# Fused attention and two expert layers: layer 2's output weights split a block earlier, the last block's pieces and the parameters tied into later groups, the first chain in two parts

## The chip, the cores and the metric

The kernel runs on one core of one Trainium2 chip. The metric is the device time of one execution in microseconds (us). Below, PE is TensorE, the matrix engine; DVE is VectorE; ACT is ScalarE; POOL is GpSimd; SP is SyncE, which issues all the DMAs here. Each engine works through its own instruction stream in order, and an instruction that waits holds up all that stand behind it on that engine.

## What is computed

Chunked attention over 4608 tokens, then two layers, each a product up to 2048 features, an elementwise function, and a product back to 512:

```python
scores = scale * np.matmul(q_c, k_c.transpose(0, 1, 2, 4, 3))   # chunks of 64
attn = softmax(scores); x = np.matmul(attn, v_c)                # x: [4608, 512]
# layer 1
h = x @ w_in;  r = np.maximum(h, 0.0);  g = s * (r * r) + b;  x = g @ w_out
# layer 2
h = x @ w_in
P = a[0] + a[1] * h + a[2] * h2 + a[3] * h3                     # h2 = h*h, h3 = h2*h
Q = 1.0 + np.abs(b[0]) * np.abs(h) + np.abs(b[1]) * h2
g = P / (Q + 1e-06);  out = g @ w_out
```

The products are kept precise by splitting a number, scaled by a power of two, into two float16 halves (hi and lo) and adding three of the four partial products.

## The kernel before

**Stages.** Tokens go in blocks: two small ones and eight of 512 in layer 1 (loop `for j in range(NFULL, NB)`), nine of 512 in layer 2. A block of layer 1 has four groups (`l1_group`), each with four slots (`l1_slot`) into which jobs from a table are put (`at(slot, fn, ...)`): attention of later blocks, pieces of x and y, and the preparation of layer 2's weights (`w2_load`, `w2_park`, then `w2_scale`). Layer 1's result of a block, y, gets its scale from the largest of its values (`y_norm`), and is then cut into seven pieces (`y_piece`, line 414 on: ACT converts to the hi half at L415, DVE subtracts for the lo half at L416; four pieces, T3, T1, T2 and T4, need a subtraction on DVE first, L402 to L411), which wait in DRAM until layer 2 fetches them (`l2_load`).

**Layer 2's output weights** (`wo2`) are decoded from float64 and parked as float32 in DRAM. In the last block of layer 1 they are fetched again (L197) into the buffers that layer 1's own weights leave, and there split into halves by ACT (L185) and DVE (L186). Eight are split in the last block and eight at the start of layer 2 (`late_jobs`).

**Layer 2** runs 36 groups of 4 blocks' quarters (`seq`). In step i TensorE makes the seven products of group i, numbered 1 to 7, in the banks bZ, bY and bC, and h is put together from them: DVE adds into h at L1070 and L1072, ACT copies from bZ at L1078 after product 3, the last. Product 3 adds into the same bank bZ that L1070 reads before it. Then the chain of the group follows: ACT makes v and e (L946, L947), DVE three operations (L955 to L957), ACT logarithm and exponential (L961, L962), DVE four operations (L970, L971, L977, L978), and g is ready. Two steps later TensorE uses g in `l2_y` (L989). The first and last chains are cut into four parts, all others are whole. After the last group of a block ACT copies four outputs (L995). Each block needs a handful of numbers first (`l2_par`, some 22 tiny DVE operations, L683 to L708).

**The order** of an engine's instructions isn't that of the code alone: a list scheduler puts them out as its own estimate of their readiness allows, unless `tc.issue_after(x)` ties the instructions on x's engine behind x. So ACT's part of a piece, for which nothing is tied, may stand elsewhere than DVE's.

Of the kernel before, what the change touches and what calls it, by code (L numbers as in the profile page):

```python
# [8 lines left out]
F32 = mybir.dt.float32  # L9
F16 = mybir.dt.float16  # L10
BF16 = mybir.dt.bfloat16
I32 = mybir.dt.int32
AF = mybir.ActivationFunctionType
ALU = mybir.AluOpType
AX = mybir.AxisListType
# [5 lines left out]
def attn_moe_moe2(ctx: ExitStack, tc: tile.TileContext, qk, v, w_in, w_out, s_in, b_in,  # L21
                  w2_in, w2_out, a2_in, b2_in, out):
    nc = tc.nc
# [4 lines left out]
    KD = DM // 128  # L28
# [47 lines left out]
    def tiny(n, nm, dt=F32):  # L76
        return y1_p.tile([128, n], dt, name=nm, tag=nm, bufs=2)
# [36 lines left out]
    class Weight:  # L114
# [34 lines left out]
        def at(self, u):  # L149
            return self.pool[u[1] % 2] if self.kind == "in" else self.pool  # L150
# [181 lines left out]
    def last(e):  # L332
        return next(i for i in reversed(nc.cur_bb.bb.instructions) if i.engine == e)
# [45 lines left out]
    def norm_bound(mx, inv, sc, nm):  # L379
        sq = tiny(KD, nm + "q")  # L380
        V.tensor_tensor(out=sq, in0=mx, in1=mx, op=ALU.mult)
        m = tiny(1, nm)
        V.tensor_reduce(out=m, in_=sq, axis=AX.X, op=ALU.add)
        tot = tiny(1, nm + "t")
        G.partition_all_reduce(tot, m, channels=128, reduce_op=bass.bass_isa.ReduceOp.add)
        pow2_root(tot, inv, sc, nm + "p")
# [177 lines left out]
    def y_norm(j2):  # L564
        m = tiny(KD, "ym")
        for dd in range(KD):
            V.tensor_reduce(out=m[:, dd:dd + 1], in_=y32[j2][:, dd, :], axis=AX.X, op=ALU.max,
                            apply_absolute_value=True)
        norm_bound(m, invy[j2], scy, "yn")
        V.tensor_scalar(out=scy, in0=scy, scalar1=0.25, scalar2=None, op0=ALU.mult)  # L570

# [11 lines left out]
    def w2_park(n):  # L583
        for m in (n, n + 1):
            w, i = park[m]
            w.decode(i, raw_p, "wf")
            V.tensor_reduce(out=am2[:, m // KF, i:i + 1], in_=w.f32[w.order[i]], axis=AX.X, op=ALU.max,
                            apply_absolute_value=True)
            w.park(i)

    quad, wsum = {}, {}

# [187 lines left out]
    for n in range(0, 2 * KF, 2):  # L780
        slot = start[2] + WS + WP * n // 2
        at(slot - 5, w2_load, n)
        at(slot, w2_park, n)
    at(start[2] + WS + WP * KF, w2_scale)

    at(start[3], l2_consts)
    at(start[NB - 1] + 2, l2_par, 0)
    at(start[NB - 1] + 3, l2_par, 1)

    if True:  # L790
        A.preload_act_table_set("natural_log_exp_and_others")
# [90 lines left out]
            return m2  # L882

        quads = [(kk, g) for g in range(2) for kk in range(2)]
        wo2.todo, wo2.cut = list(GO), list(GO)

        def l1_slot(slot, after):
            j, k = slot // KF, slot % KF
            with tc.issue_after(after.ins) if after else ExitStack():
                run_jobs(slot)  # L890
            if j == NB - 1:
                if k >= 6:
                    wo2.fetch(wo2.todo.pop(0))
                if k >= 8:
                    wo2.split(wo2.cut.pop(0))
                for n in range(28 * k // KF, 28 * (k + 1) // KF):
                    q = quads[n // 7]
                    w2_combo(q, WORD[n % 7])
                    if n % 7 == 6 and n // 7 + 1 < 4:
                        w2_fetch(quads[n // 7 + 1])  # L900
# [102 lines left out]
        T.matmul(out=prime, lhsT=wo2.hl[0][:, 0:128], rhs=wo2.hl[0][:, 0:512], start=True, stop=True)  # L1003
        N = len(seq)
        full, parts = [(0, BIG)], [(a, a + 512) for a in range(0, BIG, 512)]
        m4 = {i: [[], [], [], []] for i in range(N + 2)}
        for i in range(N):
            for q in range(4):
# [6 lines left out]
        extra = {}  # L1015

        def late_jobs():
            for fn, args in [fn for slot in sorted(jobs) for fn in jobs.pop(slot)]:
                extra.setdefault(4 + 2 * YORD.index(args[1]) if fn is y_piece else 3, []).append((fn, args))
            for n in range(len(wo2.cut)):  # L1020
                extra.setdefault(n * 2 // len(wo2.cut), []).append((lambda: wo2.split(wo2.cut.pop(0)), ()))

        last_m2 = m2_of(prev)

        def run_m4(i, slot):
            for u in m4[i][slot]:
                l2_y(*u)
            if i == 0:
                last_m2(slot)
                for _ in range((len(wo2.todo) + 3 - slot) // (4 - slot)):  # L1030
                    wo2.fetch(wo2.todo.pop(0))
                if slot == 3:
                    late_jobs()

        for i in range(N + 2):
            cur, c = i < N, i - 1
            sl = (parts if c in (0, N - 1) else full) if 0 <= c < N else []
            if cur:
                j, u = seq[i]
                if u == 1 and 1 < j + 1 < NB2:  # L1040
                    l2_par(j + 1)
                h = hs[i] = l2_p.tile([128, BIG], F32, name="h", tag="h", bufs=2)
                hq = h.rearrange("p (a s b t) -> p a b s t", a=2, s=2, b=2)
                Z, Y = new_bank(i, "Z"), new_bank(i, "Y")
                l2_product(i, "1", Z, True)
                l2_product(i, "7", Y, True)
                if u == 3 and j + 1 < NB2:
                    l2_load(j + 1)
# [29 lines left out]
                A.activation(out=hq[:, 0, 1], in_=Z, func=AF.Copy)  # L1078
            run_m4(i, 3)
            for fn, args in extra.pop(i, []):  # L1080
                fn(*args)
        assert not extra


# [33 lines left out]
```

## Time and profile before

| | |
|---|---|
| median of 3 runs | 1588.24 us (1588.1 to 1588.85) |
| the profiled execution | 1593.58 us, its span 1591.8 us |
| PE busy | 1544.3 us, 97% of the span |
| DVE busy | 1317.2 us, 83% |
| ACT busy | 962.1 us, 60% |
| mean granted clock of TensorE | 0.988 |
| all DMA | 131.43 MB, mean 83 GB/s |

How to read it: the busy shares are means over stages. Layer 1's last block is about 797 to 874 us from the span's start, the one before it about 720 to 797; layer 2 begins at 860 with its first products, and its steps are regular from about 1060 to 1580. The time before and after the span, some 1.8 us, belongs to the profiled execution's time.

### The profile page before, as it was taken

What the parts mean: (1) busy time and instruction counts of PE and PEld (TensorE: products, weight loads), DVE (VectorE), ACT (ScalarE), POOL (GpSimd) and SP (SyncE); (2) the same over time, 40 slices, a digit from 0 to 9 for tenths busy, and PEclk for the clock granted to TensorE, in tenths of its full rate; (3) what the DMA queues carried; (4) which work ended last, traced back from release to release, by engine and by line L of the source; (5) the groups of instructions that cost most, each with busy time, mean ns of one, the idle gap of its engine ahead of it and who ended that gap; (6) DMA issues with size and microseconds to landing.
All of it is one profiled execution on the core that took longest, in us unless ns stands there. A gap on an engine that the chain in (4) does not pass through costs nothing.

```text
span 1591.8 us, 29579 instructions
## 1 busy us (share of the span) xinstructions
PE 1544.3 (97%) x12501; PEld 1046.6 (66%) x12501; DVE 1317.2 (83%) x1980; ACT 962.1 (60%) x1268; POOL 24.1 (2%) x57
## 2 busy tenths in 40 slices
PE   8999999989999998999999899999999999999998
PEld 6878666656666665666666666666666666666664
DVE  7987878778878788665684999999999989888887
ACT  3565967656666565655675865555656565656564
POOL 0000000000000000000000000000000000000000
PEclk8999999999999999999999999999999999999999
DMA  7722124444534452311133020101010101010000
GB/s 275 281 76 73 47 55 127 160 139 147 152 107 156 137 166 74 87 41 54 46 121 120 14 86 27 47 27 47 27 47 28 47 27 47 28 47 34 27 27 27
DMA packets 86118, 131.43 MB, mean 83 GB/s; under 512 B 39648, under 2 KB 39648, under 8 KB 85984
## 3 DMA queue, kind: packets, MB, share of 16 engines
q1 hardware_dynamic: 85984, 129.53, 25.8%
q8 instruction: 98, 1.61, 0.4%
q14 instruction: 36, 0.29, 0.1%
HBM read 86.77 MB, written 34.34 MB: 76 GB/s over the span
## 4 chain that ended last, share of the span: by engine, by line
PE 62%; DVE 22%; ACT 7%; DMA 4%; issue 4%; POOL 0%; SPq 0%; DVEq 0%; ACTq 0%; POOLq 0%
PE y L989 18%; PE bZ L446 15%; PE y L485 11%; PE bY L446 10%; DMA raw<-in_moe_w_in_dram 2%; PE bC L446 2%; DVE bits L144 2%; PE hp L455 1%; DVE wf L145 1%; PE y L468 1%; DVE e L957 1%; DVE e L977 1%; DVE e L956 1%; DVE v L971 1%; PE sp L264 1%
## 5 line engine op out<-in xcount | busy, mean ns | idle before, releaser
L446 PEld LDWEIGHTS <-whl 128*128 128x128 f16 x5712 | 558.2, 98 | 134.7 <-issue 19.8
L446 PE MATMUL bZ<-xhl,whl 128*128 128x256 f16 x3264 | 404.2, 274 | 10.6 <-DVE h L520 7.4
L989 PE MATMUL y<-whl,g 128*128 128x512 f16 x1728 | 396.3, 379 | 4.6 <-DVE g L978 3.5
L485 PE MATMUL y<-g,whl 128*128 128x512 f16 x1536 | 353.4, 379 | 2.7 <-ACT g L493 1.8
L989 PEld LDWEIGHTS <-g 128*128 128x128 f16 x1728 | 168.6, 98 | 180.4 <-DVE g L978 5.0
L446 PE MATMUL bY<-xhl,whl 128*128 128x256 f16 x2016 | 253.0, 276 | 2.1 <-ACT sn L937 0.7
L485 PEld LDWEIGHTS <-whl 128*128 128x128 f16 x1536 | 150.4, 98 | 156.8 <-issue 3.4
L1078 ACT ACTIVATE h<-bZ 128x512 f32<-128x512 f32 x36 | 21.5, 596 | 224.8 <-PE bZ L446 173.0
L955 DVE SCALAR_TENSOR_TENSOR v<-v,c 128x2048 f32<-128x2048 f32 (+1 forms) x42 | 85.7, 2044 | 33.4 <-ACT v L946 33.4
L494 DVE TENSOR_TENSOR g<-h,g 128x1024 f16<-128x1024 f32 x64 | 78.2, 1221 | 35.9 <-ACT g L493 35.9
L522 ACT ACTIVATE h<-h 128x1024 f32<-128x1024 f32 x32 | 33.8, 1056 | 115.6 <-DVE h L520 115.6
L956 DVE TENSOR_TENSOR e<-e,h 128x2048 f32<-128x2048 f32 (+1 forms) x42 | 83.1, 1981 | 13.8 <-ACT e L947 13.8
L970 DVE SCALAR_TENSOR_TENSOR g<-e,na,r 128x2048 f16<-128x2048 f32 (+1 forms) x42 | 85.7, 2044 | 5.3 <-ACT r L962 2.2
L957 DVE SCALAR_TENSOR_TENSOR e<-e,na,h 128x2048 f32<-128x2048 f32 (+1 forms) x42 | 85.8, 2045 | 0.7
L977 DVE SCALAR_TENSOR_TENSOR e<-e,na,v 128x2048 f32<-128x2048 f32 (+1 forms) x42 | 85.6, 2042 | 0.7
L947 ACT ACTIVATE e<-h,na 128x2048 f32<-128x2048 f32 (+1 forms) x42 | 77.3, 1842 | 11.6 <-DVE g L978 11.6
L971 DVE SCALAR_TENSOR_TENSOR v<-v,g 128x2048 f32<-128x2048 f32 (+1 forms) x42 | 83.2, 1984 | 1.0
L978 DVE TENSOR_TENSOR g<-e,r 128x2048 f16<-128x2048 f32 (+1 forms) x42 | 82.9, 1976 | 0.1
L946 ACT ACTIVATE v<-h,bc 128x2048 f32<-128x2048 f32 (+1 forms) x42 | 73.8, 1759 | 15.0 <-DVE h L1072 13.9
L961 ACT ACTIVATE r<-v,c 128x2048 f32<-128x2048 f32 (+1 forms) x42 | 73.5, 1756 | 2.6 <-DVE v L955 2.6
L962 ACT ACTIVATE r<-r,c 128x2048 f32<-128x2048 f32 (+1 forms) x42 | 73.5, 1758 | 1.0
L492 ACT ACTIVATE h<-h 128x1024 f32<-128x1024 f32 x64 | 67.4, 1053 | 1.0
(189 smaller groups left out, 1820.7 us busy)
## 6 DMA issues: line engine op xcount, KB each, us to landing
qk<-in_qk_dram SPq DMA_DIRECT2D x36, 512.0 KB, 3.7
raw<-in_moe_w_in_dram SPq DMA_DIRECT2D x16, 1024.0 KB, 5.8
raw<-in_moe_w_out_dram SPq DMA_DIRECT2D x16, 1024.0 KB, 5.4
v<-in_v_dram SPq DMA_DIRECT2D x36, 256.0 KB, 2.7
out_dram<-o SPq DMA_DIRECT2D x36, 256.0 KB, 2.1
yd<-yhl SPq DMA_DIRECT2D x27, 256.0 KB, 2.0
xhl<-yd SPq DMA_DIRECT2D x27, 256.0 KB, 2.6
w2din<-wf SPq DMA_DIRECT2D x16, 256.0 KB, 2.0
```

Of the source, the lines that this page charges most:

```text
L446: T.matmul(out=b[:, s, :], lhsT=t[:, a, o:o + 128], rhs=x[pk][:, l, kk, :], start=start and s + kk + n == 0, stop=stop and s + kk + n == 4 ...
L485: T.matmul(out=ybank[j][dd], lhsT=wo1.hl[f][:, o:o + 128], rhs=g[:, l], start=(first and m == 0), stop=(last and m == 2))
L494: V.tensor_tensor(out=g[:, 1], in0=hf, in1=g[:, 0], op=ALU.subtract)
L947: A.activation(out=e, in_=hh, func=AF.Identity, scale=na[:, 3:4], bias=na[:, 2:3])
L955: V.scalar_tensor_tensor(out=v, in0=v, scalar=dlt, in1=v, op0=ALU.add, op1=ALU.mult)
L956: V.tensor_tensor(out=e, in0=e, in1=hh, op=ALU.mult)
L957: V.scalar_tensor_tensor(out=e, in0=e, scalar=na[:, 1:2], in1=hh, op0=ALU.add, op1=ALU.mult)
L970: V.scalar_tensor_tensor(out=g[:, 0], in0=e, scalar=na[:, 0:1], in1=r, op0=ALU.add, op1=ALU.mult)
L971: V.scalar_tensor_tensor(out=v, in0=v, scalar=q0c, in1=g[:, 0], op0=ALU.add, op1=ALU.mult)
L977: V.scalar_tensor_tensor(out=e, in0=e, scalar=na[:, 0:1], in1=v, op0=ALU.add, op1=ALU.subtract)
L978: V.tensor_tensor(out=g[:, 1], in0=e, in1=r, op=ALU.mult)
L989: T.matmul(out=ybank[j][t], lhsT=g[:, a, q, t * 128:(t + 1) * 128], rhs=w[:, l * 512:(l + 1) * 512], start=(u + q == 0 and m == 0), stop=( ...
```

## The change

Four things. (1) Layer 2's output weights are split once their scale is known, a block or more before the last one (`wo2_ahead`): each is loaded, split through one float32 buffer and one buffer for the halves, and stored back in its place in DRAM; later it is only fetched (`wo2_fetch`). (2) The last block's y: its four maxima are tied behind the chain's last DVE instruction in steps 8 to 11 of layer 2, its scale in 12, its seven pieces in 13, 15, ... 25. They ran in steps 1 to 6 before. (3) `l2_par`: three of the nine calls, and not two, come ahead of layer 2; the others are called at the start of a block's last group for the block after the next, tied behind the last DVE instruction traced. (4) The first chain is cut into two parts of 1024 columns in place of four of 512.

```diff
+    def wo2_ahead(i):
+        u = wo2.order[i]
+        f = raw_p.tile([128, 512], F32, name="wf", tag="wf", bufs=1)
+        nc.sync.dma_start(out=f, in_=wo2.dr[u])
+        hl = raw_p.tile([128, 512], F32, name="wb", tag="bits").bitcast(F16)
+        A.activation(out=hl[:, 0:512], in_=f, func=AF.Identity, scale=wo2.sc)
+        V.scalar_tensor_tensor(out=hl[:, 512:1024], in0=f, scalar=wo2.sc, in1=hl[:, 0:512],
+                               op0=ALU.mult, op1=ALU.subtract)
+        nc.sync.dma_start(out=wo2.dr[u].bitcast(F16), in_=hl)
...
+    for i in range(KF):
+        at(start[2] + WS + WP * KF + 2 + 5 * i // 4, wo2_ahead, i)
...
-    at(start[NB - 1] + 2, l2_par, 0)
-    at(start[NB - 1] + 3, l2_par, 1)
+    for j in range(3):
+        at(start[NB - 1] + 10 + j, l2_par, j)
...
                 if k >= 6:
-                    wo2.fetch(wo2.todo.pop(0))
-                if k >= 8:
-                    wo2.split(wo2.cut.pop(0))
+                    wo2_fetch()
...
+            for dd in range(KD):
+                extra.setdefault(8 + dd, []).append((y_max, (dd,)))
+            extra.setdefault(12, []).append((y_bound, (NB2 - 1, m)))
+            for n, p in enumerate(YORD):
+                extra.setdefault(13 + 2 * n, []).append((y_piece, (NB2 - 1, p)))
...
-            sl = (parts if c in (0, N - 1) else full) if 0 <= c < N else []
+            sl = {0: half, N - 1: parts}.get(c, full) if 0 <= c < N else []
...
-                if u == 1 and 1 < j + 1 < NB2:
-                    l2_par(j + 1)
+                if u == 3 and 3 <= j + 2 < NB2:
+                    with tc.issue_after(last(dve)):
+                        l2_par(j + 2)
...
             for fn, args in extra.pop(i, []):
-                fn(*args)
+                with tc.issue_after(last(dve)):
+                    fn(*args)
```

How this moves instructions, at three places. First ACT in layer 1's last block but one, where wb is the buffer of the new halves, yhl a piece's halves, bY and bZ TensorE's banks; now:

```order
L290 ACTIVATE ph<-e 128x512
L599 ACTIVATE wb<-wf,c_191 128x512
L415 ACTIVATE yhl<-y_9652,c_256 128x512
L513 ACTIVATE h_10059<-bY 128x2x256
L514 ACTIVATE bY<-bZ 128x512
L415 ACTIVATE yhl<-tx,c_256 128x512
L415 ACTIVATE yhl<-y_9652,c_256 128x512
L599 ACTIVATE wb<-wf,c_191 128x512 x2
L522 ACTIVATE h_10060<-h_10060 128x1024
```

The L599 rows are new; two follow each other ahead of L522.

Second DVE in layer 2 after the chain of group 13, the one in which a block's outputs are copied; before:

```order
L977 SCALAR_TENSOR_TENSOR e<-e,na,v 128x2048
L1072 TENSOR_TENSOR h<-bY,sn 128x2x256
L978 TENSOR_TENSOR g<-e,r 128x2048
L955 SCALAR_TENSOR_TENSOR v<-v,c_270 128x2048
L956 TENSOR_TENSOR e<-e,h 128x2048
```

and now (L997 is the former L978, L974 the former L955):

```order
L997 TENSOR_TENSOR g<-e,r 128x2048
L702 SCALAR_TENSOR_TENSOR c<-c_252,c_186 128x1
L706 MEMSET m 128x1
L705 TENSOR_SCALAR hb<-c 128x1
L725 TENSOR_TENSOR bc<-c_269,c 128x1
L707 TENSOR_TENSOR m<-hb,c_266 128x1
L708 TENSOR_TENSOR m<-hb 128x1
L709 TENSOR_TENSOR m<-m,c_266 128x1
L710 TENSOR_TENSOR m<-m,hb 128x1
L711 TENSOR_TENSOR m<-m,c_265 128x4
L713 TENSOR_REDUCE gm<-m 128x1
L714 TENSOR_SCALAR gm<-gm 128x1
```

Five more tiny rows follow before L974. They stood ahead of the chain with the output copies, and now stand behind it.

Third ACT around group 15's copy of bZ into h (L1078 before, L1107 now) and its v (L946, now L965); before:

```order
L1068 ACTIVATE h<-bC 128x2x256
L937 ACTIVATE sn<-bZ 128x512
L937 ACTIVATE sn<-bY 128x512
L1078 ACTIVATE h<-bZ 128x2x256
L946 ACTIVATE v<-h,bc 128x2048
```

and now:

```order
L1097 ACTIVATE h<-bC 128x2x256
L956 ACTIVATE sn<-bZ 128x512
L956 ACTIVATE sn<-bY 128x512
L415 ACTIVATE yhl<-tx,c_256 128x512
L1107 ACTIVATE h<-bZ 128x2x256
L415 ACTIVATE yhl<-y_11504,c_256 128x512
L965 ACTIVATE v<-h,bc 128x2048
```

Two conversions of y's pieces stand around the copy; tx is what DVE's L402 writes, which is tied behind the L997 of the chain before.

## Rows read from the trace of the kernel before

**Rows 1.** Busy us of each engine in five stretches, granted clock, DMA share.

```profile
core 0: us, PE busy (x) PEld busy (x) DVE busy (x) ACT busy (x) POOL busy (x), PEclk, DMA share, GB/s
...
800.00:880.00 80.00, 78.18 (x523) 50.82 (x521) 53.19 (x81) 54.52 (x82) 0.81 (x1) 1.00 0.38 122
880.00:920.00 40.00, 35.10 (x260) 25.12 (x258) 39.86 (x54) 30.94 (x42) 0.74 (x1) 1.00 0.05 14
920.00:1060.00 140.00, 134.44 (x892) 86.63 (x890) 132.76 (x110) 80.34 (x73) 0.00 (x0) 1.00 0.14 44
...
1100.00:1580.00 480.00, 480.00 (x3210) 313.78 (x3208) 435.38 (x303) 275.19 (x254) 0.00 (x0) 1.00 0.10 32
...
520.00:540.00 20.00, 18.74 (x176) 12.88 (x177) 13.99 (x31) 10.02 (x16) 0.35 (x1) 0.91 0.30 91
```

**Rows 2.** Waits of PE, 880 to 1080: us in total, times, longest.

```profile
PE y L989 <- DVE g L978: 3.5, 5, 1.0
```

**Rows 3.** Timeline of ACT in layer 2: start, us, line, [idle before].

```profile
1094.96 0.60 ACT L1078 ACTIVATE h<-bZ 128x512 f32<-128x512 f32 x1 [8.03 <-PE bZ L446]
...
1114.49 0.60 ACT L1078 ACTIVATE h<-bZ 128x512 f32<-128x512 f32 x1 [8.03 <-PE bZ L446]
```

**Rows 4.** Timeline of DVE in layer 2, 1089 to 1120.

```profile
1093.36 2.28 DVE L978 TENSOR_TENSOR g<-e,r 128x2048 f16<-128x2048 f32 x1
1097.63 2.35 DVE L955 SCALAR_TENSOR_TENSOR v<-v,c 128x2048 f32<-128x2048 f32 x1 [1.99 <-ACT v L946]
...
1111.68 0.68 DVE L1070 TENSOR_TENSOR h<-bZ,sn 128x512 f32<-128x512 f32 x1
...
1115.08 0.15 DVE L701 RECIPROCAL na<-ig 128x1 f32<-128x1 f32 x1
...
1117.60 2.34 DVE L955 SCALAR_TENSOR_TENSOR v<-v,c 128x2048 f32<-128x2048 f32 x1
```

**Rows 5.** Timeline of PE in the same step.

```profile
1112.98 1.47 PE L446 MATMUL bZ<-xhl,whl 128*128 128x256 f16 x12
```

**Rows 6.** Timeline of DVE and PE, 1039 to 1056.

```profile
1039.59 2.34 DVE L955 SCALAR_TENSOR_TENSOR v<-v,c 128x2048 f32<-128x2048 f32 x1
...
1054.38 1.47 PE L446 MATMUL bZ<-xhl,whl 128*128 128x256 f16 x12 [1.19 <-DVE h L1070]
```

**Rows 7.** Groups by form, 860 to 1060: busy us, mean ns, idle before.

```profile
L955 DVE SCALAR_TENSOR_TENSOR v<-v,c 128x2048 f32<-128x2048 f32 x9 | 21.1, 2346 | 1.4 <-ACT v L946 1.4
...
L186 DVE SCALAR_TENSOR_TENSOR whl<-wf,c,whl 128x512 f16<-128x512 f32 x8 | 6.0, 744 | 0.0
...
L567 DVE TENSOR_REDUCE ym<-y 128x1 f32<-128x512 f32 x4 | 2.7, 683 | 0.0
...
L402 DVE TENSOR_TENSOR tx<-y 128x512 f32<-128x512 f32 x1 | 0.7, 682 | 0.0
```

**Rows 8.** DMA issues: KB each, median us from issue to landing.

```profile
w2dout<-wf SPq DMA_DIRECT2D x16, 256.0 KB, 2.0
wf<-w2dout SPq DMA_DIRECT2D x16, 256.0 KB, 2.6
```

**Rows 9.** Timeline of ACT in layer 1's last block but one.

```profile
753.80 1.06 ACT L522 ACTIVATE h<-h 128x1024 f32<-128x1024 f32 x1 [4.71 <-DVE h L520]
```

**Rows 10.** Timeline of ACT and DVE after a chain with output copies.

```profile
1153.57 0.60 ACT L1078 ACTIVATE h<-bZ 128x512 f32<-128x512 f32 x1 [6.73 <-DVE h L1072]
...
1153.47 2.28 DVE L978 TENSOR_TENSOR g<-e,r 128x2048 f16<-128x2048 f32 x1
1156.24 2.35 DVE L955 SCALAR_TENSOR_TENSOR v<-v,c 128x2048 f32<-128x2048 f32 x1 [0.49 <-ACT v L946]
```

**Rows 11.** Timeline of DVE: the scale of an earlier block's y.

```profile
639.05 0.15 DVE L383 TENSOR_REDUCE yn<-ynq 128x1 f32<-128x4 f32 x1
639.70 0.15 DVE L104 TENSOR_SCALAR ynpm<-ynt 128x1 f32<-128x1 f32 x1 [0.51 <-POOL ynt L385]
```

**Rows 12.** Timeline of PE in layer 1, 508 to 524.

```profile
521.26 0.68 PE L264 MATMUL sp<-qk 64*64 64x64 f32 x18 [1.39 <-ACT x L316]
```

More of the change, by code (lines that the diff above doesn't have):

```diff
@@ L568, in y_norm, with y_bound @@
                             apply_absolute_value=True)
+        y_bound(j2, m)
+    def y_bound(j2, m):
         norm_bound(m, invy[j2], scy, "yn")
@@ L589, in w2_park, with wo2_fetch @@
             w.park(i)
+    def wo2_ahead(i):
[7 more added lines that the diff above has]
+        nc.sync.dma_start(out=wo2.dr[u].bitcast(F16), in_=hl)
+    def wo2_fetch():
+        u = wo2.todo.pop(0)
+        t = wo1_p.tile([128, 512], F32, name="whl", tag="w").bitcast(F16)
+        nc.sync.dma_start(out=t, in_=wo2.dr[u].bitcast(F16))
+        wo2.hl[u] = t
     quad, wsum = {}, {}
@@ L884, in attn_moe_moe2 @@
         quads = [(kk, g) for g in range(2) for kk in range(2)]
-        wo2.todo, wo2.cut = list(GO), list(GO)
+        wo2.todo = list(GO)
         def l1_slot(slot, after):
@@ L1005, in attn_moe_moe2 @@
         full, parts = [(0, BIG)], [(a, a + 512) for a in range(0, BIG, 512)]
+        half = [(a, a + 1024) for a in range(0, BIG, 1024)]
         m4 = {i: [[], [], [], []] for i in range(N + 2)}
@@ L1017, in late_jobs, with y_max @@
         def late_jobs():
[L1018 to L1021, printed above, removed]
+            m = tiny(KD, "ym")
+            def y_max(dd):
+                V.tensor_reduce(out=m[:, dd:dd + 1], in_=y32[NB2 - 1][:, dd, :], axis=AX.X, op=ALU.max,
+                                apply_absolute_value=True)
+            for dd in range(KD):
[3 more added lines that the diff above has]
+                extra.setdefault(13 + 2 * n, []).append((y_piece, (NB2 - 1, p)))
+            jobs.clear()
         last_m2 = m2_of(prev)
@@ L1030, in run_m4 @@
                 for _ in range((len(wo2.todo) + 3 - slot) // (4 - slot)):
-                    wo2.fetch(wo2.todo.pop(0))
+                    wo2_fetch()
                 if slot == 3:
```

## The prediction

> **What bounds the kernel now.** I read the busy time by stretches first. There the reader sees four stretches [rows 1]: the last layer-1 block (800 to 880) with TensorE busy 78.18 of 80 us, the first 40 us of layer 2 with 35.10 of 40, the next 140 us with 134.44 of 140, and 1100 to 1580 with 480.00 of 480. TensorE sets the end, so a change is worth what it takes out of, or puts into, TensorE's idle time. What there is to win before 1060 is 1.82 + 4.90 + 5.56 = 12.3 us; VectorE is full there (39.86 of 40, 132.76 of 140), and the waits name it [rows 2]. Then I read the steady stretch instruction by instruction, because the change adds work there, and "480 of 480" does not say how near to waiting TensorE is. One group of layer 2 takes 19.53 us (the copy at 1094.96, the next at 1114.49 [rows 3]). Its loop: ScalarE copies product 3 out of PSUM (L1078), makes v, VectorE starts its chain with L955 2.67 us after that copy began (1097.63), reaches the add L1070 at 1111.68, done at 1112.36 [rows 4], and TensorE's product 3 of the next group, which accumulates into the bank that this add reads, starts at 1112.98 [rows 5]. So the loop has **0.62 us** to spare in 19.53. Whatever delays L955 by more stops TensorE, at once and for good. The trace holds one such case: at 1039.59 L955 began 1.9 us later than usual behind the tiny parameter operations, and TensorE stood 1.19 us at 1054.38, waiting for L1070 [rows 6].
>
> **What it removes.** VectorE loses, between 875 and 985, eight weight splits of 0.744 us, four maxima of 0.683 and the last block's seven pieces with their subtractions (about 0.74 and 0.68 each) [rows 7]: 6.0 + 2.7 + 7.9 = 16.6 us. In the first chain alone 4 maxima and 4 splits go (5.7 us), but the second half's v is queued on ScalarE behind four y copies, which I put at 3 us of VectorE idle that was none before; by that the second group's adds come some 2.6 to 3 us earlier. I take 1.8 us of the 4.90 as left: **-3.1**. In the next 140 us VectorE then has a chain of some 17 us against 19.5 of TensorE and leads; I take 0.3 of the 5.56 as left: **-5.3** (bounds 0 and -5.56). In the last block eight splits on each engine go; half of 1.82 I leave, since its first stall follows a load of the first layer's weights: **-0.9** (0 to -1.82). Together -9.3.
>
> **What the split ahead adds.** Sixteen times a load of 256 KB, 0.71 us of ScalarE, 0.74 of VectorE, a store, through one buffer each. Load and store both start behind VectorE's half and land after 2.6 and 2.0 us [rows 8], so one step needs about 4.1 us before the next can start. Steps stand about five microseconds apart, mostly in pauses in which ScalarE waits for VectorE or TensorE anyway, as the 4.71 us at 753.80 [rows 9]. The tightest place is the first one shown of the order: two steps stand side by side in that pause, 0.71 + 0.74 + 2.6 + 0.71 = 4.8 us in 4.7. Nothing of this is under a stall in the trace (TensorE is busy 80 of 80 there), and the loss is bounded by 0 and, if each step held TensorE by what it has over half a pause, 16 x 0.9 = 14 us. Nearest to the pause is a small loss: **+1.0**.
>
> **What moves into the steady loop.** Here I find the change's real price; nothing covers it beyond 0.62 us.
> (a) The parameters of a block (six of them now inside layer 2, one each four groups) stood, in the steady part before, ahead of the chain whose output copies make it late: there 2.52 us of tiny operations from 1115.08 to 1117.60 [rows 4] filled the pause of 2.0 us, 0.5 too long, inside the 0.62. Now they stand right behind that late chain. After such a chain VectorE has no pause: its last L978 begins at 1153.47, 0.10 before the copy at 1153.57, and the next L955 at 1156.24 [rows 10], only 0.5 us after L978's end (2.2 us after its start). 2.52 us there delay L955 by 2.52 - 0.57 = 1.95, and TensorE by 1.95 - 0.62 = **1.3 us, six times: 7.8**. This is the case of 1054.38 again, within 0.1.
> (b) The scale of the last block's y: VectorE does seven tiny operations with a GpSimd reduction among them (0.65 us from L383 to L104 [rows 11], 0.19 from each other one to the next, as the parameter operations; some 1.75 in all), and ScalarE's first conversion, which waits for the last of them, stands ahead of v. v then starts 0.6 (the chain's end) + 1.75 + 0.65 (the conversion) = 3.0 us after the copy began instead of 0.6: 2.4 late, minus 0.62: **1.8**.
> (c) The four pieces with a subtraction (T3, T1, T2, T4). The subtraction is tied behind the chain's last instruction on VectorE, so it starts 0.6 us after the copy should (1115.08 against 1114.49), and takes 0.68 [rows 3, 4, 7]. ScalarE's conversion of it stands ahead of that copy, so ScalarE waits for it: 0.6 + 0.7 + 0.65 = 1.9 us late. Minus 0.62 that is **1.3 each**. T3 and T4 have the conversion of a second piece ahead of v, 0.6 more; T3, T1 and T4 come one group after a delayed chain, which has used up the 0.62: 0.6 more. So 2.5, 1.9, 1.3, 2.5: **8.2**. The maxima (0.68 in a pause of 2.0) and the three pieces without a subtraction stay under 0.62: 0, and up to 0.6 each where another delay has used it.
> Bounds of (a) to (c): 0, if the pauses before L955 grow for a reason I don't see, and 24, if none of the 0.62 is there.
>
> **The sum.** -3.1 - 5.3 - 0.9 + 1.0 + 7.8 + 1.8 + 8.2 = +9.5 us. The profiled execution took 1593.58 us; with it the sum is 1603.1. It lies 5.3 us above the median of the runs shown, 1588.24, for which I forecast **1597.7 us**, slower by 0.6%. The chains at the end are as before, so nothing is lost or won in the tail.
>
> **A rule on the clock.** At 521.26 TensorE resumed after 1.39 us [rows 12], and in the 20 us around it the granted clock was 0.91 of full speed; in the 40 us from 880, with 4.90 us idle, it stayed at 1.00 [rows 1]. At 0.91 a stretch of 20 us holds 1.8 us less work. The Trainium skill (TensorE: Matmul & The Clock Gate, Why this matters for your kernels) says that long idle gaps between bursts of matmuls put the clock back to half. By that rule and the row at 521 each of the eleven stalls of (a) to (c) could cost another 1.8 us, the sum would be 1603.1 + 19.8 for the profiled execution; by the row at 880 nothing is added. The stalls here lie between long runs of matmuls, as at 880, so I add nothing.
>
> **Rivals.**
> 1. The waits of (a) to (c) don't come about: the loop opens because VectorE, freed of 16.6 us, leads. Then the sum is -9.3 + 1.0 = -8.3: 1579.9, faster. For it: VectorE is busy only 435.38 of 480 in the steady part. Against: the 0.62 us does not hang on the load but on the loop copy, v, chain, add, in which VectorE never leads, since L955 waits for v [rows 4].
> 2. Half of it: only the parameters (a), or only the pieces (b, c), stop TensorE. -8.3 + 7.8 or + 10.0: 1587.7 to 1589.9, no change. For it: the two have separate causes. Against: both use the same 0.62.
> 3. The split ahead blocks ScalarE, in addition: two copies of a PSUM bank for TensorE stand behind each step in the order; it decides from the point where a step's wait is longer than ScalarE's pause. 1597.7 + 13 = 1610.7. Against: the pauses of 4.7 us.
> 4. The change doesn't do what it says: VectorE stays the bound at the start of layer 2, for the chain in two parts starts later than one in four, and only -3 of the 9.3 comes. 1604 with the rest as forecast.
> 5. The clock of the rule above falls behind the longer stalls: 1597.7 + up to 19.8.
>
> **How the numbers follow.** Forecast 0.66; rival 1 0.13; rival 2 0.10; rival 3 0.04; rival 4 0.04; rival 5 0.03. The forecast's own range is 1592 to 1602 (its costs 4 to 5 us either way, the gains 2). For 8 in 10 I reach down through rival 2, to 1586.5, and up to 1603; rival 1 and the far ends of 3 and 5 are left out. A measurement of this kernel can tell about 0.2%, 3.2 us, from no change. Slower by more: 0.66 with 0.02 off for its low end, rivals 3, 4 and 5: 0.75. Within: most of rival 2 and that low end: 0.10. Faster: rival 1 and a little of 2: 0.15.
>
> **What would show it.** In the profile after, TensorE's idle time in the last block and the next 180 us should fall from 12.3 to some 3 us, and 1100 to 1580 should no longer be full: stalls "bZ waits for DVE h" of 1.2 to 2.6 us, six of them one to two groups behind the tiny operations, and ScalarE's conversion of tx or y idle ahead of its copy of bZ for more than 8 us. No split should stand in layer 2, and the stretch 640 to 800 should lose about 1 us. I am wrong if the steady stretch stays full, above all if bZ's add comes in time in the groups with a subtraction.

## The result, and the profile after

The changed kernel took 1610.6 us (median of 4, 1605.37 to 1614.12) against 1588.55 us before: a ratio of 1.0131, 95% interval 1.0097 to 1.0165. A second series (below) gave 1.0122 [1.0104, 1.0140]. So it is slower, by some 20 us; the forecast was slower by 9.5, and 1610.6 lies above its range and above its 8 in 10. The profiled execution took 1608.57 us.

Busy us of each engine by stretches in the changed kernel, columns as in [rows 1]:

```profile
680.00:720.00 40.00, 37.42 (x348) 24.96 (x347) 24.76 (x51) 25.59 (x39) 0.72 (x2) 0.96 0.29 88
800.00:880.00 80.00, 75.88 (x509) 49.60 (x508) 45.13 (x68) 47.54 (x68) 0.81 (x1) 1.00 0.37 119
880.00:920.00 40.00, 37.77 (x277) 26.75 (x275) 33.31 (x25) 26.69 (x29) 0.00 (x0) 1.00 0.06 20
920.00:1060.00 140.00, 136.11 (x914) 88.83 (x912) 127.62 (x86) 78.77 (x70) 0.00 (x0) 1.00 0.10 34
1100.00:1580.00 480.00, 467.05 (x3142) 307.06 (x3140) 429.85 (x311) 268.78 (x248) 0.39 (x1) 1.00 0.11 36
```

Against [rows 1]: the stretch that was full, 1100 to 1580, now has 12.95 us of idle TensorE. The first two stretches of layer 2 have 2.23 and 3.89 idle where they had 4.90 and 5.56: less gained than forecast. The last layer-1 block has become worse, 4.12 for 1.82. And 680 to 720, which had 0.11 us idle before, has 2.58 and a granted clock of 0.96.

TensorE's waits in the steady stretch (us in total, times, longest):

```profile
PE bZ L446 <- DVE h L1099: 10.6, 8, 1.7
PE y L1008 <- ACT o L1014: 1.6, 1, 1.6
PE bC L446 <- ACT bC L1085: 0.7, 2, 0.3
```

The first row is the wait that the prediction named: product 3 for the add that was L1070 and is L1099. How it comes about stands in the timelines of steps 12 and 15 (start, us, line, idle before):

```profile
1116.01 0.15 DVE L104 TENSOR_SCALAR ynpm<-ynt 128x1 f32<-128x1 f32 x1 [0.59 <-POOL ynt L385]
...
1119.61 2.35 DVE L974 SCALAR_TENSOR_TENSOR v<-v,c 128x2048 f32<-128x2048 f32 x1 [2.68 <-ACT v L965]
...
1114.48 0.60 ACT L1107 ACTIVATE h<-bZ 128x512 f32<-128x512 f32 x1 [8.03 <-PE bZ L446]
1116.96 0.72 ACT L415 ACTIVATE yhl<-y,c 128x512 f16<-128x512 f32 x1 [1.88 <-DVE c L573]
1117.59 1.99 ACT L965 ACTIVATE v<-h,bc 128x2048 f32<-128x2048 f32 x1
...
1134.40 1.47 PE L446 MATMUL bZ<-xhl,whl 128*128 128x256 f16 x12 [1.73 <-DVE h L1099]
...
1178.05 0.72 ACT L415 ACTIVATE yhl<-tx,c 128x512 f16<-128x512 f32 x1 [10.36 <-DVE tx L402]
1178.67 0.58 ACT L1107 ACTIVATE h<-bZ 128x512 f32<-128x512 f32 x1
...
1196.58 0.60 PE L446 MATMUL bZ<-xhl,whl 128*128 128x256 f16 x4 [1.73 <-DVE h L1099]
```

The copy at 1114.48 is on time (1114.49 in [rows 3]). Behind it ScalarE stands 1.88 us for the scale of y, with v queued behind the conversion: v starts 3.1 us after the copy began (forecast 3.0), the chain 5.1 (2.67 to 3.1 in [rows 3, 4]), and 15 us later TensorE stands 1.73. At 1178.05 the conversion of T3 has held ScalarE for 10.36 us, of which 8 are its usual pause; the copy behind it is late, and so is the next product 3.

To see where the rest went I compare starts of the same instruction in both traces: product y of layer 1 (L485) numbers 860, 1080, 1380 and 1535 (counted from 0), and ScalarE's copy L1078 (now L1107) of groups 12 and 28. Before these stand at 579.83, 685.19, 813.81, 878.90, 1114.49 and 1427.13; the columns are what each stretch takes more than before, in us.

| kernel | 860 to 1080 | to 1380 | to 1535 | to group 12 | to group 28 |
|---|---|---|---|---|---|
| changed | +1.6 | **+5.3** | +2.5 | -4.3 | **+14.65** |
| changed, second run | +2.8 | +6.4 | +1.8 | -4.3 | +14.6 |
| split ahead alone | +0.1 | +5.4 | +0.9 | -1.7 | +0.2 |
| split ahead undone | +0.4 | 0.0 | -1.1 | -2.4 | +14.6 |
| parameters undone | +0.9 | +7.5 | +1.7 | -5.2 | +10.1 |
| late pieces undone | +1.5 | +6.1 | +1.6 | -1.8 | +3.7 |
| late pieces mended | -0.4 | +5.1 | +1.6 | -4.3 | +4.6 |
| before, late pieces mended alone | +0.5 | 0.0 | -0.4 | -2.7 | 0.0 |

The parts add up: 1.61 + 5.25 + 2.47 - 4.25 + 14.65 = 19.73 us. After group 28 all of these run alike (164.65 to 164.69 us to the end). Before number 860 nothing of the change runs, and there executions differ by chance: it stands at 574.74 and 580.82 in two executions of the changed kernel. That is why whole kernels are compared by the medians of many executions, and stretches by the table.

### The profile page after: what moved, and what is told of

Its sections match the earlier page's. It is cut to its first block, busy times and chain, and to the rows that moved or that the text cites. A ratio compares the mean times of both kernels' runs of the same rounds, so it can differ in the third digit from the quotient of the medians.

```text
span 1606.5 us, 29595 instructions
## 1 busy us (share of the span) xinstructions
PE 1543.8 (96%) x12501; PEld 1045.4 (65%) x12501; DVE 1315.7 (82%) x1966; ACT 958.5 (60%) x1260; POOL 24.8 (2%) x57
## 3 DMA queue, kind: packets, MB, share of 16 engines
q8 instruction: 98, 1.61, 0.4%
## 4 chain that ended last, share of the span: by engine, by line
PE 43%; DVE 32%; ACT 12%; issue 6%; DMA 6%; POOL 0%; SPq 0%; DVEq 0%; POOLq 0%; ACTq 0%
PE bZ L446 10%; PE y L1008 10%; PE y L485 10%; PE bY L446 7%; DVE g L989 3%; DVE v L990 2%; DVE e L976 2%; DMA raw<-in_moe_w_in_dram 2%; DVE e L975 2%; DVE v L974 2%; DVE g L997 2%; DVE e L996 2%; DVE bits L144 2%; DMA raw<-in_moe_w_out_dram 1%; DVE wf L145 1%
## 5 line engine op out<-in xcount | busy, mean ns | idle before, releaser
L485 PE MATMUL y<-g,whl 128*128 128x512 f16 x1536 | 353.9, 380 | 1.8 <-ACT g L493 1.8
L485 PEld LDWEIGHTS <-whl 128*128 128x128 f16 x1536 | 150.6, 98 | 156.4 <-issue 3.1
L1107 ACT ACTIVATE h<-bZ 128x512 f32<-128x512 f32 x36 | 21.4, 594 | 211.5 <-PE bZ L446 164.4
L974 DVE SCALAR_TENSOR_TENSOR v<-v,c 128x2048 f32<-128x2048 f32 (+2 forms) x40 | 85.4, 2136 | 44.3 <-ACT v L965 44.3
L522 ACT ACTIVATE h<-h 128x1024 f32<-128x1024 f32 x32 | 33.8, 1055 | 106.3 <-DVE h L520 106.3
L975 DVE TENSOR_TENSOR e<-e,h 128x2048 f32<-128x2048 f32 (+2 forms) x40 | 82.8, 2073 | 14.8 <-ACT e L966 14.8
L989 DVE SCALAR_TENSOR_TENSOR g<-e,na,r 128x2048 f16<-128x2048 f32 (+2 forms) x40 | 85.2, 2137 | 5.2 <-ACT r L981 2.4
L976 DVE SCALAR_TENSOR_TENSOR e<-e,na,h 128x2048 f32<-128x2048 f32 (+2 forms) x40 | 85.4, 2138 | 1.1
L996 DVE SCALAR_TENSOR_TENSOR e<-e,na,v 128x2048 f32<-128x2048 f32 (+2 forms) x40 | 85.2, 2135 | 0.7
L990 DVE SCALAR_TENSOR_TENSOR v<-v,g 128x2048 f32<-128x2048 f32 (+2 forms) x40 | 82.8, 2077 | 0.9
L997 DVE TENSOR_TENSOR g<-e,r 128x2048 f16<-128x2048 f32 (+2 forms) x40 | 82.5, 2069 | 0.1
L965 ACT ACTIVATE v<-h,bc 128x2048 f32<-128x2048 f32 (+2 forms) x40 | 73.1, 1831 | 14.5 <-DVE h L1101 13.6
L966 ACT ACTIVATE e<-h,na 128x2048 f32<-128x2048 f32 (+2 forms) x40 | 76.5, 1914 | 6.9 <-DVE g L997 6.9
L980 ACT ACTIVATE r<-v,c 128x2048 f32<-128x2048 f32 (+2 forms) x40 | 73.1, 1830 | 8.6 <-DVE v L974 8.6
```

The source lines that it names most:

```text
L485: T.matmul(out=ybank[j][dd], lhsT=wo1.hl[f][:, o:o + 128], rhs=g[:, l], start=(first and m == 0), stop=(last and m == 2))
L966: A.activation(out=e, in_=hh, func=AF.Identity, scale=na[:, 3:4], bias=na[:, 2:3])
L974: V.scalar_tensor_tensor(out=v, in0=v, scalar=dlt, in1=v, op0=ALU.add, op1=ALU.mult)
L975: V.tensor_tensor(out=e, in0=e, in1=hh, op=ALU.mult)
L976: V.scalar_tensor_tensor(out=e, in0=e, scalar=na[:, 1:2], in1=hh, op0=ALU.add, op1=ALU.mult)
L989: V.scalar_tensor_tensor(out=g[:, 0], in0=e, scalar=na[:, 0:1], in1=r, op0=ALU.add, op1=ALU.mult)
```

## Experiments

Ratios are to the kernel before, run on the same chip, with 95% intervals.

**The four parts, one at a time.** First the split ahead put into the kernel before, by itself.

```diff
     at(start[2] + WS + WP * KF, w2_scale)
+    for i in range(KF):
+        at(start[2] + WS + WP * KF + 2 + 5 * i // 4, wo2_ahead, i)
...
-                    wo2.fetch(wo2.todo.pop(0))
-                if k >= 8:
-                    wo2.split(wo2.cut.pop(0))
+                    wo2_fetch()
```

> The kernel before with part 1 alone: the sixteen output weights of layer 2 split a block ahead and fetched later; parameters, last block's y and first chain as before. Theory A (the split ahead is what the forecast undersized): in the trace of the changed kernel TensorE's start of groups slips by 7.3 us between 637 and 879, by 3.5 at 699 (a stall of 2.0, then half clock) and by 1.2 and 2.4 at 741 and 821 to 841. So this kernel loses 5 to 7 us there; the sixteen splits gone from the last block and the start of layer 2 give back 2 to 4 of VectorE's 12 us: 1590 to 1594 us, and the stalls at the scores after a split recur. Rival B (layer 1's slip is a difference between two executions, the split ahead costs 1 us as forecast): 1583 to 1586 us, faster than before.

Measured 1.0024 [1.0013, 1.0035], +3.8 us (5.3 by the medians), and +5.4 in its stretch, with a stall at the scores: theory A. The start of layer 2 gave back only 1.7, for the 2 to 4 expected, and the last block, with eight splits fewer on each engine, took 0.9 more. The opposite, taking the split ahead out of the changed kernel:

```diff
-    for i in range(KF):
-        at(start[2] + WS + WP * KF + 2 + 5 * i // 4, wo2_ahead, i)
...
+                if k >= 8:
+                    wo2.split(wo2.cut.pop(0))
```

> The changed kernel with part 1 undone: the output weights are split in the last block and in the first two steps of layer 2 again, everything else as in the changed kernel. Theory A: 5 to 7 us come back in layer 1, 1 to 3 are lost at the start of layer 2 to the splits: 1604 to 1607 us against 1610.6, and no stall at the scores near 700. Rival B: layer 1 has nothing to give back, the splits cost VectorE 6 us at the start of layer 2: 1610 to 1615.

Measured 1.0059 [1.0043, 1.0075]: 10 to 11 us better than the changed kernel by the ratios, 8.3 by the table, where 3.6 to 6.6 were expected (5 to 7 in layer 1, less 1 to 3 at the start of layer 2). The stretch to number 1380 is as before to 0.04 us, the next one, up to 1535, gave back 3.5, and the start of layer 2 lost 1.8. Next the parameters back in place:

```diff
-                if u == 3 and 3 <= j + 2 < NB2:
-                    with tc.issue_after(last(dve)):
-                        l2_par(j + 2)
+                if u == 1 and 1 < j + 1 < NB2:
+                    l2_par(j + 1)
```

> The changed kernel with part 3 undone: two calls of the parameters ahead of layer 2, the others in the second group of a block, not tied. Theory A: the stalls at product 3 one group behind the parameters go (0.50, 0.91, 1.03, 1.03, 0.64 and 1.04 us in the trace of the changed kernel, with what follows them 5 to 6): 1604.5 to 1606 us. Rival C (the delay belongs to the chains with output copies, whatever stands behind them): the stalls stay, 1609 to 1611.

1.0065 [1.0051, 1.0079]. The stalls behind the parameters go (14.65 falls to 10.1, and 1.0 more is gained before group 12): 5.5 us, theory A. By the ratios the gain is larger, 9 to 10 us; single traces and medians agree only within some 4 us, since layer 1 varies. Then maxima, scale and pieces put back untied, so that they run at the start of layer 2 again (from 880 to 961 in its trace):

```diff
+            for fn, args in [fn for slot in sorted(jobs) for fn in jobs.pop(slot)]:
+                extra.setdefault(4 + 2 * YORD.index(args[1]) if fn is y_piece else 3, []).append((fn, args))
...
             for fn, args in extra.pop(i, []):
-                with tc.issue_after(last(dve)):
-                    fn(*args)
+                fn(*args)
```

> The changed kernel with part 2 undone: maxima, scale and pieces of the last block's y in steps 1 to 16 of layer 2 as before, not tied. Theory A: the stalls behind the scale (1.73) and behind T3, T1, T2 and T4 (2.07, 1.73, 1.64, 2.06) go, 9.2 us; the maxima and pieces take VectorE's time at the start of layer 2 again, 10.6 us of work of which 2 to 5 show: 1603 to 1606 us. Rival D (the start of layer 2 is VectorE's to the full): 1609 to 1612, all of it given back.

1.0043 [1.0027, 1.0059]: 11.0 us go in the steady part, 2.5 come back at the start (8.5 together, 12 to 14 by the ratios). Theory A; rival D falls, VectorE's 10.6 us of work at the start cost 2.5.

**The sum again, the wait of the pieces, and the loads.** The changed kernel itself, unchanged:

> The changed kernel itself, beside the others and beside the kernel before on one chip, since its first four executions spread over 8.7 us. Theory A (the pieces of the trace add up: 1.6 near 610, 5.3 from 685 to 814, 2.5 to the end of layer 1, -3.8 at the start of layer 2, 14.6 in the steady part): 20 us over the kernel before, 18 to 23. Theory E (executions differ in layer 1, and the first comparison caught slow ones): 12 to 16 us over it.

1.0122 [1.0104, 1.0140], +20.3 us: the parts add up to the time. Now the four subtractions stand a group earlier and the conversions in ScalarE's pause, with every instruction kept:

```diff
+                mark = last(nc.scalar.engine)     # behind the copies of products 1 and 7
...
+                if p in ("T3", "T1", "T2", "T4"):
+                    extra.setdefault(12 + 2 * n, []).append((piece_sub, ...))
                 extra.setdefault(13 + 2 * n, []).append((y_piece, (NB2 - 1, p)))
...
-                with tc.issue_after(last(dve)):
+                with tc.issue_after(last(dve)), tc.issue_after(mark):
```

> The changed kernel with one thing mended: the subtraction of T3, T1, T2 and T4 stands one step earlier, and ScalarE's conversion of every piece is tied behind the copies of product 7 and 1, in the 8 us in which ScalarE waits for product 3. VectorE's and ScalarE's work is the same to the last instruction. Theory A (the wait of ScalarE for a subtraction costs the time, not the work): the stalls of 1.73 behind the scale and of 2.1, 1.7, 1.6 and 2.1 behind the pieces go, 8 to 10 us below the changed kernel. Rival F (1.4 us more of VectorE and 0.7 of ScalarE in a step are what delays the chain): at most 2 us below it.

1.0045 [1.0028, 1.0062], 12.6 us below the changed kernel by the medians, 10.0 by the table's last column. But for 0.2 us, only stalls behind the parameters are left in its steady stretch, though VectorE and ScalarE are busier there than in the changed kernel (437.77 and 280.11 us for 429.85 and 268.78):

```profile
PE bZ L466 <- DVE h L1122: 3.8, 4, 1.0
PE y L1028 <- ACT o L1034: 0.2, 1, 0.2
```

So the price was ScalarE's wait, not the work; rival F falls. The same mended pieces put into the kernel before, alone (maxima in steps 7, 7, 9 and 10, scale in 11, subtractions two steps ahead of their pieces):

> The kernel before with part 2 alone, mended: the last block's maxima, scale and pieces tied behind later chains, the subtraction a step or more ahead of the conversion, the conversion in ScalarE's long pause; splits, parameters and first chain as before. Theory A: no stall in the steady part, 1.7 to 2.5 us of the first 140 us of layer 2 gained: 1.5 to 3 us faster than before. Rival F: the pieces cost their stalls wherever they stand, 6 to 9 us slower. Rival G (the first steps of layer 2 are VectorE's work to the full, 10.6 us of which go): 8 to 10 us faster.

**0.9977 [0.9968, 0.9987], faster than before by 3.7 us** (3.9 by the medians, 2.6 by the table; 1.5 to 3 were expected): the one version that beats both kernels, though a second one with the same pieces, below, did not repeat the gain. Its stretches:

```profile
880.00:920.00 40.00, 35.66 (x262) 25.21 (x260) 38.19 (x41) 28.11 (x37) 0.00 (x0) 1.00 0.07 24
920.00:1060.00 140.00, 136.05 (x903) 87.78 (x901) 130.18 (x106) 81.20 (x70) 0.00 (x0) 1.00 0.11 36
...
1100.00:1580.00 480.00, 480.00 (x3198) 312.71 (x3197) 440.03 (x314) 274.83 (x257) 0.00 (x0) 1.00 0.11 36
```

VectorE has 4.65 us more in 1100 to 1580 than before, and TensorE is full. With 10.6 us of VectorE's work out of the start, 2.7 are gained: rivals F and G fall.

For the split ahead, one load of four weights in place of one each:

```diff
-        f = raw_p.tile([128, 512], F32, name="wf", tag="wf", bufs=1)
-        nc.sync.dma_start(out=f, in_=wo2.dr[u])
+        f = stage[0][:, i % 4, :]          # four weights loaded by one earlier job
```

> The kernel before with the split ahead (as in the first run, 3.8 us slower than before), its loads changed alone: four parked weights are fetched at once into the buffer that layer 2's raw weights left, and each split reads one of them. Theory A (ScalarE and behind it VectorE stand for the load: 16.5 us of ScalarE's idle time ahead of seven of the sixteen splits, 8.1 of VectorE's): the slip between 685 and 814 falls from 5.3 to under 2 us, and the kernel is within 1 us of before or faster by up to 2. Rival H (the 0.72 of ScalarE and 0.75 of VectorE themselves push the copies that TensorE waits for): the slip stays at 4 to 5.5, 3 to 4 us slower than before.

1.0013 [0.9998, 1.0029]; the stretch to 1380 takes +3.2 for +5.4. Between the theories: the stalls of 0.97 and 1.15 at 744 and 766, which the split ahead alone has, go, and the one at the scores stays (1.74 us, with half clock behind it).

**The first chain, and other slots for the split.** The first chain in two parts, by itself:

```diff
-            sl = (parts if c in (0, N - 1) else full) if 0 <= c < N else []
+            sl = {0: half, N - 1: parts}.get(c, full) if 0 <= c < N else []
```

> The kernel before with part 4 alone: the first chain in two parts in place of four. Theory A (by the traces so far, kernels with two parts are 0.8 us ahead of the one with four at the fourth copy of layer 2): 0 to 1 us faster, no difference a measurement can tell. Rival I (the first part is ready later, product and output products of the first groups wait for it): 1 to 2 us slower.

0.9990 [0.9978, 1.0003], -1.5 us up to group 12: no difference that the timing can tell; rival I falls. The staged split with three slots left free:

```diff
-        at(start[2] + WS + WP * KF + 2 + 5 * i // 4, wo2_ahead, i)
+        at(start[2] + WS + WP * KF + (2 + i if i < 4 else 6 + i), wo2_ahead, i)
```

> The kernel before with the split ahead and its staged loads (the run before this one of that kind: 3.2 us of slip between 685 and 814, all of it behind one stall of 1.74 at 702), and three slots of the table left free after the fourth split, so that none stands on ScalarE or VectorE between the x pieces at 683 and the read-out of x at 703. Theory A (a split costs where it stands ahead of a copy that has no slack, here the read-out of x, and nothing elsewhere): no stall at 702, slip under 1 us, 1 to 3 us faster than the staged one. Rival H (each split pushes by its own 0.7, the stall only collects it): the stall shows at the next scores, at 723, slip 2.5 to 3.5, no faster.

1.0043 [1.0026, 1.0059], the stretch +6.8. **My theory failed here**: the stall at 702 shrank to 0.53, but one of 2.27 came at 758 and one of 1.26 at 780. "Nothing elsewhere" was wrong; nor did the stall move to the next scores at 723, as rival H had it. ScalarE and VectorE at 758:

```profile
758.28 0.72 ACT L602 ACTIVATE wb<-wq,c 128x512 f16<-128x512 f32 x1 [4.30 <-DMA w2dout<-wb]
...
759.03 0.75 DVE L603 SCALAR_TENSOR_TENSOR wb<-wq,c,wb 128x512 f16<-128x512 f32 x1 [3.57 <-ACT wb L602]
759.70 0.68 DVE L520 TENSOR_TENSOR h<-bZ,sn 128x512 f32<-128x512 f32 x1
```

The split waits for the store of the one before, VectorE's half 3.57 us for ScalarE's, and L520, for which TensorE waits, behind it. (At 780 two sums of the input weights stand ahead of L519 and L520.) Mended pieces and first chain in two parts together:

> The mended late pieces (3.9 us faster than before) with the first chain in two parts as well: splits and parameters as before. Theory A: 0 to 1 us below the one with four parts, 3.5 to 5 us faster than before. Rival I: 1 to 2 us above it.

0.9997 [0.9983, 1.0010], no difference to before, where 3.5 to 5 us faster were expected. By the trace it should equal the mended pieces alone (-3.5 and -2.7 up to group 12); the two ratios, of different series, lie 3.2 us apart, and what separates them isn't settled (its profile stood 6 us later at number 860). So the gain of the mended pieces rests on one series. All parts, mended:

> All parts with what the runs taught: split ahead from staged loads with the gap at 702, late pieces with the subtraction early and ScalarE's part in its pause, parameters as before, first chain in two parts. Theory A: slip of the split ahead under 1, last layer-1 block 0.9 to 2.5 later as in every kernel with the split ahead, first 180 us of layer 2 4.3 to 5.3 earlier, steady part as before: 2 to 4 us faster than before, about as the kernel with mended pieces alone. Rival G (VectorE's 16.6 us leave the start at last, with nothing else in the way): 6 to 8 us faster.

1.0009 [0.9996, 1.0023]: the 2 to 4 us expected did not come. The split ahead still costs 4.9 (under 1 was expected) and 2.1, the start gains 5.7, the steady part is as before (-0.1). Rival G falls once more.

**What the split ahead costs: work, traffic or waiting.** Open was which; three kernels took one away each. Only the work, on a buffer of zeros:

```diff
+        if i == 0:
+            V.memset(dummy[0], 0.0)
+        A.activation(out=hl[:, 0:512], in_=dummy[0], func=AF.Identity, scale=wo2.sc)
+        V.scalar_tensor_tensor(out=hl[:, 512:1024], in0=dummy[0], scalar=wo2.sc, in1=hl[:, 0:512], ...)
```

> The kernel before, with the sixteen pairs of instructions of the split ahead in its slots, but on a buffer of zeros that is there from the start, with no load and no store; the real splits stay where they are in the kernel before. Theory A (the waiting is the price): slip between 685 and 814 under 1.5 us, kernel 0 to 2 us slower than before. Rival H (the work is the price): slip 4 to 5.5, kernel 4 to 6 us slower.

1.0017 [0.9998, 1.0036]; the stretch +1.9, nearly all of it one stall of 1.86 at the scores: a little over theory A's 1.5, far under rival H's 4. Only the transfers:

```diff
+        nc.sync.dma_start(out=f, in_=wo2.dr[u])
+        nc.sync.dma_start(out=wo2.dr[u], in_=f)
```

> The kernel before, with the sixteen loads and stores of the split ahead in its slots and no instruction of ScalarE or VectorE between them; the real splits stay. Theory A and rival H: slip between 685 and 814 under 0.5 us, no difference to before. Rival J (the traffic delays the loads and transposes of layer 1): slip of 2 or more.

1.0012 [0.9997, 1.0026]; the stretch -0.1: the traffic costs nothing there, rival J falls. Staged loads, and two buffers for the halves in turn:

```diff
-        hl = raw_p.tile([128, 512], F32, name="wb", tag="bits").bitcast(F16)
+        hl = raw_p.tile([128, 512], F32, name="wb", tag=("bits", "wf")[i % 2]).bitcast(F16)
```

> The staged split ahead (slip 3.2, ScalarE idle 8.5 us ahead of its halves and VectorE 4.5 behind them) with two buffers for the halves in turn, so that no split waits for the store of the one before. Theory A: ScalarE's idle time ahead of its halves under 4, VectorE's under 3, slip 1.5 to 2.5. Rival H: slip 3 or more as with one buffer.

1.0015 [0.9998, 1.0032]; the stretch +3.3. ScalarE's wait went, VectorE's fell to 3.3 (under 3 was expected), but the slip did not fall below the staged one's 3.2, as rival H had it: one stall of 1.89, and half clock behind it. The two halves of the split in four kernels, 655 to 815 (busy us, mean ns, idle before and what ended it), of the changed kernel, of the one with other slots, of the staged one with two buffers, and of the work alone:

```profile
L600 DVE SCALAR_TENSOR_TENSOR wb<-wf,c,wb 128x512 f16<-128x512 f32 x16 | 12.0, 749 | 8.1 <-ACT wb L599 8.1
...
L599 ACT ACTIVATE wb<-wf,c 128x512 f16<-128x512 f32 x16 | 11.5, 719 | 16.5 <-DMA wf<-w2dout 16.5
```

```profile
L603 DVE SCALAR_TENSOR_TENSOR wb<-wq,c,wb 128x512 f16<-128x512 f32 x16 | 12.0, 748 | 11.7 <-ACT wb L602 11.7
L602 ACT ACTIVATE wb<-wq,c 128x512 f16<-128x512 f32 x16 | 11.5, 718 | 15.4 <-DMA w2dout<-wb 5.4 <-DVE e L276 4.0 <-DMA wq<-w2dout 3.7
```

```profile
L603 DVE SCALAR_TENSOR_TENSOR wb<-wq,c,wb 128x512 f16<-128x512 f32 x16 | 12.0, 748 | 3.3 <-ACT wb L602 3.3
L602 ACT ACTIVATE wb<-wq,c 128x512 f16<-128x512 f32 x16 | 11.4, 712 | 0.0
```

```profile
L599 DVE SCALAR_TENSOR_TENSOR wb<-wf,c,wb 128x512 f16<-128x512 f32 x16 | 12.0, 748 | 3.3 <-ACT wb L598 3.3
L598 ACT ACTIVATE wb<-wf,c 128x512 f16<-128x512 f32 x16 | 11.4, 712 | 0.0
```

The work is the same in all. VectorE's wait for ScalarE's half is 8.1, 11.7, 3.3 and 3.3 us, ScalarE's own wait 16.5, 15.4, 0.0 and 0.0, the stretch +5.3, +6.8, +3.3 and +1.9. So the price has three parts: 1.9 for the one stall that the work alone makes; 1.4 to 1.6 of half clock behind it in some executions (below); and the rest, by subtraction some 1.8 us in the changed kernel and 3.5 in the split ahead alone (5.4 - 1.9, no half clock), for standing behind a half that waits for a load or a store. The rows show it on either engine: VectorE at 758 above, and ScalarE in the split ahead alone, where L596 is its half, L522 follows only behind it, and TensorE waits for L527:

```profile
761.95 0.72 ACT L596 ACTIVATE wb<-wf,c 128x512 f16<-128x512 f32 x1 [5.72 <-DMA wf<-w2dout]
...
766.91 1.47 PE L446 MATMUL bY<-xhl,whl 128*128 128x256 f16 x12 [1.15 <-ACT h L527]
```

The two waits rise and fall together in these kernels, so the runs don't say how much of the rest each makes.

## Why the prediction was wrong

**By stretches.** The forecast put 0, +1.0, -0.9, -5.8 (its -8.4 and two of the six parameter delays) and +15.2 us into the five columns of the table above; +1.6, +5.3, +2.5, -4.3 and +14.65 came. The steady part was right, and all of the miss lies ahead of it.

**What was right.** Sign and main mechanism: the 0.62 us, and each of the late stalls. The parameters cost 0.50, 0.91, 1.03, 1.03, 0.64 and 1.04 at TensorE, 5.2 for the 7.8 forecast; the scale 1.73 for 1.8; T3, T1, T2 and T4 2.07, 1.73, 1.64 and 2.06 (0.34 of the first and last is a wait for ScalarE's copy to bC), 7.5 for 8.2. T2's 1.64 came by another path than forecast: its conversion held ScalarE in a group with output copies, and TensorE's output product waited for one of these (L1014), not product 3 for the add. From group 12 to 28, where four of the six parameter delays lie, the forecast was 5.2 + 1.8 + 8.2 = 15.2, measured 14.65. (Of these 1.7 are not in the idle rows; the ends of matmuls are modelled.) Half of it, rival 2, is out, and rival 1 with it.

**The step that failed most: what the split ahead adds, +1.0.** It measured +5.3 and +6.4. I fitted a step of 4.8 us into ScalarE's pause of 4.7 and took a small loss. But a pause of ScalarE isn't one of VectorE: VectorE's half stands in its order ahead of the adds L519 and L520, and waits there for ScalarE's half, which waits for the load. And a pause is no room for a half that waits in it for a load longer than it lasts, as at 761.95 above. In the changed kernel, before the stall at the scores:

```profile
686.18 0.72 ACT L599 ACTIVATE wb<-wf,c 128x512 f16<-128x512 f32 x1 [1.45 <-DMA wf<-w2dout]
...
686.94 0.75 DVE L600 SCALAR_TENSOR_TENSOR wb<-wf,c,wb 128x512 f16<-128x512 f32 x1 [0.86 <-ACT wb L599]
687.61 0.68 DVE L519 TENSOR_TENSOR h<-bY,sn 128x512 f32<-128x512 f32 x1
...
689.11 0.68 DVE L520 TENSOR_TENSOR h<-bZ,sn 128x512 f32<-128x512 f32 x1
...
689.84 0.38 PE L446 MATMUL bZ<-xhl,whl 128*128 128x256 f16 x2 [0.59 <-DVE h L520]
...
701.07 1.07 PE L264 MATMUL sp<-qk 64*64 64x64 f32 x18 [2.00 <-ACT x L316]
702.07 2.68 PE L446 MATMUL bY<-xhl,whl 128*128 128x256 f16 x12
```

L520 late by the split (0.86 + 0.75) makes product 3 wait 0.59, the next conversions stand later, and at 701.07 the scores wait 2.00 for ScalarE's read-out of x (L316). The work alone, with no stall at product 3, makes a stall of 1.86 there: most of that one is the work's. "TensorE 80 of 80" said, as in the steady stretch, nothing of how near to waiting it was; I looked for the margin there and not here. Rival 3 had the place and, with copies standing behind a step that waits longer than ScalarE's pause, a part of the cause; it left out VectorE, and had 13 us.

**The last layer-1 block, -0.9,** measured +0.9 to +2.5 in every kernel with the split ahead, and -1.1 in the changed kernel without it. With the splits gone the order moves halves of the input weights (L640) and their sums (L626) ahead of L520, and TensorE stands 1.69 at 839; at 821 it stands 1.53 for ScalarE's copy L527, behind such a half (L639) that waits for VectorE's sums. That is read from the trace and was not tried by itself, so the cause stays open.

**The start of layer 2, -8.4.** With the parameters put back it measured -5.2. I read VectorE's 39.86 of 40 and TensorE's wait for its g as "VectorE's work is the bound". VectorE's own waits from 880 to 1060, first of the kernel before, then of the changed one:

```profile
DVE e L956 <- ACT e L947: 4.3, 3, 2.2
DVE v L955 <- ACT v L946: 1.4, 1, 1.4
```

```profile
DVE v L974 <- ACT v L965: 11.8, 6, 3.7
DVE e L975 <- ACT e L966: 6.5, 3, 2.2
```

Freed of 16.6 us, VectorE waits 18.3 instead of 5.7, and TensorE still waits for g:

```profile
PE y L1008 <- DVE g L997: 2.5, 4, 1.1
```

That is 3.5 in [rows 2]. What is left is the loop copy, v, chain, g, output products, copy, late from its first turn, which gets back in each turn only its small slack; no run took that late start away, so this is argued and not shown. What the runs show is that VectorE's work is not what most of the idle time hangs on: the mended pieces take 10.6 us of it off, and 2.7 are gained. So rival 4 was right that most of the 9.3 would not come, and wrong on why: it had VectorE as the bound.

**From 860 to 1080 the changed kernel took 1.6 and 2.8 more.** I gave that nothing. But the kernel with transfers alone, which has nothing else there, took 2.3 more, and others -0.6 to +1.5, among them three that hold the third parameter call as well (-0.4, +0.4 and +1.5); this stretch holds a stall of mostly 4 to 5 us at the scores and half clock behind it. So no cost of the third call shows, and what made the 1.6 stays open.

**The clock.** Nothing was added for it in the steady stretch, and its granted clock stayed at 1.00 through all stalls there: by the Trainium skill's rule (TensorE: Matmul & The Clock Gate, Why this matters for your kernels), that long idle gaps between bursts of matmuls put the clock back to half, gaps of 1.73 us were not long ones. In layer 1 the clock did fall behind stalls hardly longer, of 1.74 to 2.00 us, in some executions and not in others, as the last section shows.

## What to carry to other kernels

A stretch in which the bound engine is 100% busy may have a margin of tenths of a microsecond in any loop: look for it before putting even "hidden" work there, on each engine that the new work queues on, and put an instruction that must wait behind the ones that others wait for. Where a producer is full and its consumer waits, taking work off the producer may only give it idle time: here 16.6 us less work left VectorE waiting 12.6 us more.

## What was not expected of the hardware

The same stall ahead of the same matmuls has two outcomes. TensorE stood 1.74 to 2.00 us ahead of the scores near 700 in nine executions. The twelve matmuls of bY behind it took 2.53 to 2.73 us in six of them (the changed kernel twice, with the parameters undone, with the late pieces undone, the staged ones with one and with two buffers; granted clock 0.91 to 0.96 in the 20 us from 690 to 710, that is, a while at 1.2 GHz) and 1.48 in three at the full 2.4 GHz (split ahead alone, late pieces mended, work alone; 1.00). What decides it no run here shows. With the split ahead alone:

```profile
705.92 0.68 PE L264 MATMUL sp<-qk 64*64 64x64 f32 x18 [2.00 <-ACT x L316]
706.53 1.48 PE L446 MATMUL bY<-xhl,whl 128*128 128x256 f16 x12
```

against 1.07 and 2.68 above. Where it fell, it cost 1.4 us more by the stretches of two kernels with nearly the same stall (staged with two buffers 3.3, work alone 1.9), 1.6 by the rows (from the scores' second start to the end of bY 3.68 us for 2.09).
